# Pair sums held in a PSUM bank, and two gate results in one bank

## Chip, cores and metric

The kernel runs on one core of a Trainium2 chip. The metric is the device time of one execution in microseconds (us); lower is better. The work is split over TensorE (PE, with its weight loads as PEld), VectorE (DVE), ScalarE (ACT), GpSimd (POOL) and the DMA queue that SyncE issues (SP).

## What is computed

Three stages follow one another: a recurrent attention over 768 steps (4 batches, 8 heads, 48 wide), a soft mixture of 8 experts with 32 slots, and a bilinear layer. The last two, cut to what matters here:

```python
slot_out = ...                                # 32 slots x 384, from the experts
x = c @ slot_out                              # c: 3072 tokens x 32 slots (softmax)
a, b = x @ w_a, x @ w_b                       # 384 -> 1536
return (a * b) @ w_out                        # 1536 -> 384, 3072 tokens
```

## The kernel before, in words

A token's x is a mix of 32 slots, so `a*b` of a token is a quadratic form in its 32 weights `c`. The kernel therefore never makes `a` and `b` for 3072 tokens. It makes them for the 32 slots, forms the products of pairs of slots, multiplies those by `w_out` once, and at the end multiplies each block of 128 tokens' pair weights by that small result.

**Gates.** `Gates.products` (line 852) multiplies the experts' output by the two weight matrices in three thirds m = 0, 1, 2. `Gates.turned` (line 869) transposes one third on TensorE into a PSUM tile `pt` (256 numbers per partition), which ScalarE copies into SBUF (line 876), with a small VectorE copy of the first 16 columns (line 877). Each of the three tiles has a bank of its own, tags `g0`, `g1`, `g2` in banks 5, 6 and 7 (line 1279).

**Pair sums.** There are 12 of them, f = 0 to 11, four from each third. Each is a chain over four engines:

- `Sums.pairs(f)` (line 906) forms two products of 128x512 at line 914: `z` on VectorE, from the gate's PSUM tile and its SBUF copy, and `z2` on POOL, from the SBUF copy alone (for f = 0 both are on VectorE). `z` has three SBUF buffers, `z2` two.
- `Sums.add(f)` (line 938): VectorE adds `z2` to `z`, in place in SBUF.
- `Sums.round(f)` (line 943): ScalarE rounds the sum to the short format, `zh` (three buffers).
- `Sums.second(f)` (line 949): VectorE subtracts `zh` from the sum, which gives the remainder `zl` (two buffers).
- `Sums.product(f)` (line 963): TensorE adds twelve 128x384 matmuls (`zh` and `zl` with the two parts of `w_out`) into four PSUM banks.

The order on each queue is the order in which the program emits it. `Sums.run` (line 966) emits for i = 0 to 11: `pairs(i+2)`, `second(i+1)`, `add(i+2)`, `round(i+2)`, what stands beside it, then `product(i)`. The first two sums are started by hand (lines 1286 to 1302). What stands beside (line 1309) is, for i = 2, 4, 6, three small POOL products (`Sums.rest`, lines 925 to 927); for i = 3, 5, 7 their eight small matmuls (line 933); for i = 7, 8, 9, 11 a step of `Pairs.rest` (ScalarE copies at line 1001, then POOL adds at lines 1004 and 1005, ScalarE copies at line 1008); for i = 6, 9 the VectorE product at line 1050 and for i = 7, 10 its split (ScalarE line 1062, VectorE lines 1063 and 1064), which prepare the first two blocks of tokens.

**Output.** `Pairs.take` (lines 1022 to 1028) splits the sums' result, and `Pairs.product` (line 1090) makes 24 blocks of 128 tokens with 13 matmuls each (lines 1098, 1101, 1102), in banks 5, 6 and 7, with a copy (line 1105) and a store (line 1106).

Of the kernel before, what the change touches and what calls it, by code (L numbers as in the profile page):

```python
# [7 lines left out]
F32 = mybir.dt.float32  # L8
# [5 lines left out]
ALU = mybir.AluOpType  # L14
# [38 lines left out]
class Slots:  # L53


    def __init__(self, pool):
        self.pool, self.n = pool, 0
# [12 lines left out]
class Carve:  # L70
# [5 lines left out]
    def add(self, area, *spec):  # L76
        if isinstance(area, list):
            for a, s in zip(area, spec):
                self.add(a, *s)
            return self  # L80
        o = 0
        for tag, n, bufs in spec:
            for _ in range(bufs):
                self.views.setdefault(tag, []).append(area[:, o:o + n])
                o += n
        assert o <= area.shape[1], (o, spec)
        return self
# [693 lines left out]
def experts(nc, sh, k, siT, scale, sb, ps, wq, soT, step):  # L781
# [14 lines left out]
    for r in range(2):  # L796
        for j in range(4):
            e = 4 * r + j
            w = wq.tiles[e]
            hp = ps.tile([128, 256], F32, tag="p", name="hp")  # L800
            for kb in range(KB):
                for q in range(4):
                    nc.tensor.matmul(out=hp[32 * q:32 * q + NS, :], lhsT=siT[:, kb, :], rhs=w[q][:, kb, :],
                                     start=(kb == 0), stop=(kb == KB - 1))
            wq.done(e)
            h = sb.tile([128, 256], F32, tag="h", name="h")
            nc.scalar.activation(out=h, in_=hp, func=ACTF.Relu, scale=scale)
            if late:
                turned(*late.pop())
            late.append((r, j, h))  # L810
            step(e)
# [32 lines left out]
class Gates:  # L844
# [2 lines left out]

    def __init__(self, nc, sh, k, sb, soT, ws):
        self.nc, self.sh, self.k, self.sb, self.soT, self.ws = nc, sh, k, sb, soT, ws
        self.a, self.p, self.g = {}, {}, {}  # L850

    def products(self, ps, m):

# [15 lines left out]
    def turned(self, ps, m):  # L869
        nc, NS = self.nc, self.sh.NS  # L870
        a = self.a.pop(m)
        self.p[m] = pt = ps.tile([128, 2, 4, NS], F32, tag=f"g{m}", name="pt")
        for i in range(2):
            nc.tensor.transpose(out=pt[:, i], in_=a[:, i, :], identity=self.k["ident"])
        self.g[m] = g = self.sb.tile([128, 2, 4, NS + 16], F32, tag="gate", name="gate")
        nc.scalar.activation(out=g[:, :, :, 0:NS], in_=pt, func=ACTF.Copy)
        nc.vector.tensor_copy(out=g[:, :, :, NS:NS + 16], in_=pt[:, :, :, 0:16])
# [8 lines left out]
class Sums:  # L886
# [47 lines left out]
                             start=(m == 0), stop=(m == 2))  # L934

    def add(self, f):
        z, z2 = self.st[f]
        self.nc.vector.tensor_tensor(out=z, in0=z, in1=z2, op=ALU.add)

    def round(self, f):  # L940
        z, _ = self.st[f]
# [246 lines left out]
def kernel(  # L1188
# [39 lines left out]
    def post(k, siT, scale, wq, slots, wab, wo_sb, banks, sb, pairs, chore):  # L1228
        ps = banks.again(p=(4, 5, 6, 7), wm=(0, 1))
        chore = chore(ps)  # L1230
        free = [(5, 5), (6, 6), (7, 7), (8, 8), (9, 9), (11, 10), (3, 14), (4, 15)]
        sums = Sums(nc, sh, k, wo_sb, sb)

        warm = k["ident"].bitcast(BF16)

        def keep(n):

            if n:
                t = ps.tile([128, 256], F32, tag="wm", name="warm")
                for _ in range(n):  # L1240
                    nc.tensor.matmul(out=t, lhsT=warm[:, 0:128], rhs=warm, start=True, stop=True)

        def step(e, last=None):

            while free and wq.used > free[0][1]:
                i = free.pop(0)[0]
                if i in (6, 7, 8):
                    sums.rooms += [[s[:, j * DM:(j + 1) * DM].bitcast(F32R) for j in range(2)]
                                   for s in slots.quarters(i)]
                elif i == 9:  # L1250
                    sb.add(slots.take(i), ("cab", 2304, 1), ("f", 640, 1))
                    pairs.ncab, pairs.nf = 1, 1
                elif i == 11:
                    sb.add(slots.take(i), (("ga", 384, 2),), (("gate", 384, 2),), (("gate", 384, 1), ("o", 384, 1)),
                           (("o", 384, 2),))
                elif i == 3:
                    sb.add(slots.take(i), ("cab", 2304, 1), ("f", 640, 1))
                    pairs.ncab, pairs.nf = 2, 2
                else:
                    s = slots.quarters(i)  # L1260
                    pairs.rooms += [s[0:2], s[2:4]]
            if last:
                keep(KEEP[e])
                last()
            if e == 1:
                pairs.moe.keep(sh.NG - 1, ps, "p")
            if e > 6:
                sums.split()
                sums.split()
            if e in (8, 13):  # L1270
                next(chore, None)
            if not last:
                keep(KEEP[e])

        sb.add(pairs.moe.acc_room[:, 0:KB * sh.NS], ("soT", KB * sh.NS, 1))
        soT = sb.tile([128, KB, sh.NS], F32, tag="soT", name="soT")
        experts(nc, sh, k, siT, scale, sb, ps, wq, soT, step)
        pairs.loads(soT)
        ps = banks.again(p=(0, 1, 2), g0=(5,), g1=(6,), g2=(7,))
        sb.add(slots.take(10), ("r1", 1536, 1))  # L1280
        sb.add(slots.take(0), ("zh", 512, 3), ("zl", 512, 2), ("tr", 384, 1))
        sb.add(slots.take(1), ("z", 512, 3), ("z2", 512, 2), ("zr", 64, 2))
        gates = Gates(nc, sh, k, sb, soT, wab)
        sums.gates = gates
        pairs.blank()
        part = [gates.products(ps, m) for m in range(3)]
        next(part[0])
        next(part[0])
        next(part[1])
        gates.turned(ps, 0)  # L1290
        sums.pairs(0)
        next(part[1])
        next(part[2])
        sums.add(0)
        gates.turned(ps, 1)
        next(part[2])
        sums.round(0)
        sums.pairs(1)
        sums.second(0)
        sums.add(1)  # L1300
        gates.turned(ps, 2)
        sums.round(1)
        ps = banks.again(tp0=(0,), tp1=(1,), tp2=(2,), tp3=(3,), tp4=(4,))
        tp = [ps.tile([128, DM], F32, tag=f"tp{m}") for m in range(5)]
        sb.add(wab[0].rearrange("p k f -> p (k f)"), ("f", 640, 2), ("cab", 2304, 1))
        pairs.ncab, pairs.nf = 3, 4
        last = pairs.rest(tp[4])

        def beside(n):
            sums.split()  # L1310
            if n in (2, 4, 6):
                sums.rest(n // 2 - 1)
            if n in (3, 5, 7):
                sums.rest_product(n // 2 - 1, tp[4])
            if n in (7, 8, 9, 11):
                next(last, None)
            if n in LATER:
                getattr(pairs, LATER[n])()

        sums.run(tp, beside)  # L1320
        for _ in last:
            pass
        sb.add(slots.take(2), ("th", 1536, 1), ("tl", 1536, 1))
        pairs.take(tp)
        ps = banks.again(yo=(5, 6, 7))
        pairs.ahead(2)
        pairs.product((0, 1), ps)
        for n in range(2, pairs.n):
            pairs.ahead(2)
            pairs.product((n,), ps)  # L1330
# [3 lines left out]
    with tc.manual_schedule(), ExitStack() as fast:  # L1334
# [3 lines left out]
        banks = Banks(fast.enter_context(tc.tile_pool(name="banks", bufs=1, space=PSUM)),  # L1338
                      tp=TPB, A=AB, y=(5, 6), misc=(7,))
        ps = banks  # L1340
# [46 lines left out]
        for n in range(NU + 1):  # L1387
# [5 lines left out]
            if n >= 1:  # L1393
                g = (n - 1) // 2
# [6 lines left out]
            if 3 <= n < NU:  # L1401
                if n % 2:
                    g = (n - 3) // 2
# [6 lines left out]
            if PRE[0] <= n < PRE[1]:  # L1410
                m = 4 * NPRE * (n + 1 - PRE[0]) // (PRE[1] - PRE[0]) - 4 * NPRE * (n - PRE[0]) // (PRE[1] - PRE[0])
# [9 lines left out]
            if n == NU - 1:  # L1421
# [7 lines left out]
        rest(sb2, slots)  # L1429
        pairs = Pairs(nc, sh, k, moe, sb2, out)  # L1430
        post(k, siT, scale, wq, slots, wab, wo_sb, banks, sb2, pairs,
             lambda ps: range_flag(nc, sh, k, pool, moe, att, flag, ps))

    val = nc.values_load(flag, min_val=0, max_val=1)
    with tc.If(val > 0):
        with ExitStack() as slow:
# [5 lines left out]
            banks = Banks(slow.enter_context(tc.tile_pool(name="sbanks", bufs=1, space=PSUM)), tp=(0, 1), misc=(2, 3, 4), p=(5, 6, 7))  # L1442
# [23 lines left out]
            rest(sb2, slots)  # L1466
            pairs = Pairs(nc, sh, k, moe, sb2, out)
            post(k, siT, scale, wq, slots, wab, wo_sb, banks, sb2, pairs, lambda ps: iter(()))


# [28 lines left out]
```

## Time and profile before

| | us |
|---|---|
| median of 3 runs | 392.18 (391.66 to 392.22) |
| the profiled execution | 391.77 |
| its span, first to last instruction | 390.0 |
| busy: PE / PEld / DVE / ACT / POOL | 336.3 / 265.6 / 308.2 / 227.5 / 181.2 |

The span is what the rows of the trace divide; the profiled execution's own time is 1.77 us longer than its span, and 0.41 us below the median. Of the span, the stretch from 0 to 288 us is attention and experts, 288 to 328.5 the gates and pair sums, and from there to the end the output. A row of the timeline gives start, duration, engine, line, operation, output and inputs, shapes, and in brackets how long the engine had been idle and what released it.

### The profile page before, as it was taken

The page shows a single profiled execution, that of the slowest core. Times are in us where ns is not written, and L with a number is a line of the kernel's source. Part 1 is how long each engine was busy: PE and PEld are TensorE (multiplying, and loading weights), DVE is VectorE, ACT ScalarE, POOL GpSimd, SP SyncE. Part 2 cuts the span into 40 slices and gives each one's busy share as a digit, 9 for nine tenths or more (in the row PEclk, how much of TensorE's full clock was granted, in tenths as well). Part 3 has the DMA queues.
Part 4 walks back from the last instruction along what each step waited for, and adds up shares of the span by engine and source line. Part 5 has one row for each costly group of instructions (what it writes and reads, how often), then busy time and mean ns, then how long its engine had stood idle before and what let it go on. Part 6 is the DMA issues. An engine that isn't in the chain of part 4 may idle for free.

```text
span 390.0 us, 9985 instructions
## 1 busy us (share of the span) xinstructions
PE 336.3 (86%) x3634; PEld 265.6 (68%) x3634; DVE 308.2 (79%) x616; ACT 227.5 (58%) x672; POOL 181.2 (46%) x224
## 2 busy tenths in 40 slices
PE   7595979988878979878879988899989969999993
PEld 3364767767756858757757776554457759998993
DVE  2476999999999998999999975425349979877850
ACT  4277687795976957966966855335232235544451
POOL 5263776676666566675666651000026734222200
PEclk9689889999999869989989989999999999999999
DMA  7669797879979668979668998799859100899422
GB/s 124 123 116 261 158 210 192 203 151 235 255 152 218 183 118 201 253 160 231 164 127 190 257 294 255 229 366 376 288 130 215 24 0 2 229 270 305 142 90 69
DMA packets 138634, 73.75 MB, mean 189 GB/s; under 512 B 105328, under 2 KB 133104, under 8 KB 138576
## 3 DMA queue, kind: packets, MB, share of 16 engines
q1 hardware_dynamic: 137424, 69.48, 71.2%
q0 software_dynamic: 1152, 3.54, 2.7%
q8 instruction: 31, 0.51, 0.6%
q14 instruction: 27, 0.22, 0.2%
HBM read 67.68 MB, written 5.31 MB: 187 GB/s over the span
## 4 chain that ended last, share of the span: by engine, by line
DVE 49%; PE 24%; DMA 13%; issue 6%; SPq 4%; ACT 3%; POOL 0%; DVEq 0%; ACTq 0%; POOLq 0%
DMA s<-in_moe_w_dram 8%; DVE s L534 8%; DVE s L529 7%; PE yo L1098 6%; DVE s L583 6%; DVE s L712 5%; DVE wab L714 4%; DVE s L551 3%; PE yo L1101 3%; SPq L489 3%; DVE wo L714 2%; PE tp L579 2%; DVE s L683 2%; PE tp L963 2%; PE y L680 2%
## 5 line engine op out<-in xcount | busy, mean ns | idle before, releaser
L505 PE MATMUL tp<-ident,s 128*128 128x128 f32 x288 | 50.0, 298 | 7.7 <-ACT s L593 3.8
L579 PE MATMUL tp<-s,s 64*128 64x128 f32 x384 | 37.2, 298 | 18.9 <-DVE s L610 9.5
L579 PEld LDWEIGHTS tp<-s,s 64*128 64x128 f32 x384 | 30.2, 197 | 24.0 <-issue 21.7
L554 POOL TENSOR_TENSOR s<-s,s 128x384 f32<-128x384 f32 x32 | 37.4, 1190 | 18.5 <-DVE s L551 18.5
L505 PEld LDWEIGHTS tp<-ident,s 128*128 128x128 f32 x288 | 33.5, 148 | 18.1 <-issue 6.0
L647 ACT ACTIVATE s<-s,s 128x48 f32<-128x48 f32 x192 | 45.7, 324 | 0.2
L547 POOL TENSOR_TENSOR s<-s,s 128x384 f32<-128x384 f32 x30 | 36.7, 1238 | 15.7 <-DVE s L534 10.0
L583 DVE TENSOR_TENSOR s<-tp,s 128x384 f32<-128x384 f32 x64 | 32.4, 545 | 9.4 <-PE tp L579 9.2
L529 DVE TENSOR_TENSOR_SCAN s<-s,s 128x387 f32<-128x387 f32 x32 | 33.1, 1072 | 7.0 <-ACT s L510 7.0
L1098 PE MATMUL yo<-s,s 128*128 128x384 f32 x192 | 37.8, 338 | 0.4 <-DVE s L1063 0.4
L534 DVE TENSOR_TENSOR_SCAN s<-s,s 128x387 f32<-128x387 f32 x32 | 35.0, 1121 | 0.5
L680 PEld LDWEIGHTS y<-s,s 128*64 128x64 f32 x768 | 29.0, 156 | 9.0 <-issue 8.7
L1098 PEld LDWEIGHTS yo<-s,s 128*128 128x128 f32 x192 | 33.7, 188 | 1.2 <-DVE s L1063 1.0
L963 PE MATMUL tp<-s,s 128*128 128x384 f32 x144 | 29.8, 358 | 5.2 <-DVE s L949 4.5
L680 PE MATMUL y<-s,s 128*64 128x48 f32 x768 | 33.2, 243 | 0.0
L963 PEld LDWEIGHTS tp<-s,s 128*128 128x128 f32 x144 | 25.9, 198 | 10.0 <-DVE s L949 7.0
L512 ACT ACTIVATE s<-tp 128x384 f32<-128x384 f32 x64 | 30.2, 488 | 2.5 <-PE tp L505 1.7
L717 POOL TENSOR_TENSOR wab<-wab,s 128x384 int32<-128x384 int32 x24 | 27.8, 1160 | 6.3 <-DVE wab L714 2.8
L1105 ACT ACTIVATE s<-yo 128x384 f32<-128x384 f32 x24 | 11.8, 493 | 28.0 <-PE yo L1102 11.9
L1106 POOL DMA_DIRECT2D out_dram<-s x18 | 9.9, 553 | 33.9 <-ACT s L1105 32.0
L712 DVE TENSOR_SCALAR s<-s 128x384 uint32<-128x384 uint32 x36 | 23.2, 644 | 2.9 <-ACT wab L704 2.9
L620 POOL TENSOR_TENSOR s<-s,pc_all 64x288 f32<-64x288 f32 (+1 forms) x32 | 21.2, 663 | 8.1 <-DVE s L610 6.9
(190 smaller groups left out, 738.9 us busy)
## 6 DMA issues: line engine op xcount, KB each, us to landing
s<-in_moe_w_dram SPq DMA_DIRECT2D x64, 384.0 KB, 5.9
s<-in_w_dram SPq DMA_DIRECT2D x48, 96.0 KB, 3.5
s<-in_k_dram SPq DMA_DIRECT2D x48, 96.0 KB, 5.0
s<-in_r_dram SPq DMA_DIRECT2D x48, 96.0 KB, 3.2
s<-in_v_dram SPq DMA_DIRECT2D x48, 96.0 KB, 3.4
s<-in_moe_w_a_dram SPq DMA_DIRECT2D x12, 384.0 KB, 3.9
s<-in_moe_w_b_dram SPq DMA_DIRECT2D x12, 384.0 KB, 4.1
s<-in_moe_w_out_dram SPq DMA_DIRECT2D x12, 384.0 KB, 3.7
```

Of the source, the lines that this page charges most:

```text
L505: nc.tensor.transpose(out=pt[:, c, :], in_=t[:, c, 2 * p:2 * p + 2, :].rearrange("p h d -> p (h d)"), identity=ident)
L529: nc.vector.tensor_tensor_scan(out=P[:, hs[p]], data0=wt[:, hs[p]], data1=self.lo, initial=0.0, op0=ALU.mult, op1=ALU.max)
L534: nc.vector.tensor_tensor_scan(out=suf[:, hs[p]][:, ::-1], data0=wt[:, o + 1:o + H + 1][:, ::-1], data1=d1[:, hs[p]][:, ::-1], initial=0.0 ...
L547: (nc.gpsimd if n else nc.vector).tensor_tensor(out=part(suf, p, 1), in0=part(suf, p, 1), in1=plain(kT, p), op=ALU.mult)
L554: nc.gpsimd.tensor_tensor(out=plain(rT, p), in0=plain(rT, p), in1=plain(kT, p), op=ALU.mult)
L579: nc.tensor.matmul(out=aps[hh][:, c, :], lhsT=K[64 * hh:64 * hh + 64, o + 1:o + 1 + C], rhs=R[64 * hh:64 * hh + 64, o:o + C], start=True, ...
L583: nc.vector.tensor_tensor(out=a, in0=aps[hh], in1=self.mask.unsqueeze(1).to_broadcast([128, 3, C]), op=ALU.mult)
L647: nc.scalar.activation(out=av[:, c, h], in_=V[:, c, h, 0:D], func=ACTF.Copy, scale=a0[:, c, h // 2, h % 2:h % 2 + 1])
L680: nc.tensor.matmul(out=yp[th, c, hh, :], lhsT=am[p, hh][:, c, th], rhs=V[:, c, 2 * p + hh, :], start=False, stop=c == 2 and hh == 1)
L712: nc.vector.tensor_scalar(out=raw[:, :, 1], in0=raw[:, :, 1], scalar1=0x80000000, scalar2=None, op0=ALU.bitwise_and)
L963: nc.tensor.matmul(out=tp[m], lhsT=a[:, m * 128:(m + 1) * 128], rhs=b, start=first and i == 0, stop=last and i == 2)
L1098: nc.tensor.matmul(out=y, lhsT=a[:, m, :], rhs=self.th[:, m, :], start=m == 0 and a is fh, stop=False)
```

## The change

The sum of the two products is written by `add` to a PSUM tile `zs` of one bank (7) in place of the SBUF buffer `z`; `round` and `second` read it there. To free that bank, the gates' tiles of m = 0 and m = 1 become two halves of one tile in bank 5, and that of m = 2 moves to bank 6.

```diff
@@ Gates.turned
-        self.p[m] = pt = ps.tile([128, 2, 4, NS], F32, tag=f"g{m}", name="pt")
+        if m % 2 == 0:
+            self.room = ps.tile([128, 2, 2, 4, NS], F32, tag=f"g{m}", name="pt")
+        self.p[m] = pt = self.room[:, m % 2]
@@ Sums.add
         z, z2 = self.st[f]
-        self.nc.vector.tensor_tensor(out=z, in0=z, in1=z2, op=ALU.add)
+        zs = self.ps.tile([128, 512], F32, tag="z", name="zs")
+        self.nc.vector.tensor_tensor(out=zs, in0=z, in1=z2, op=ALU.add)
+        self.st[f] = zs, None
@@ post
-        ps = banks.again(p=(0, 1, 2), g0=(5,), g1=(6,), g2=(7,))
+        ps = banks.again(p=(0, 1, 2), g0=(5,), g2=(6,), z=(7,))
...
-        sums.gates = gates
+        sums.gates, sums.ps = gates, ps
```

## Rows read from the trace of the kernel before

**Rows 1.** Busy time by stretch: us (instructions) of PE, PEld, DVE, ACT, POOL; clock, DMA.

```profile
291.90:328.50 36.60, 31.77 (x169) 26.50 (x170) 33.07 (x42) 12.75 (x23) 22.02 (x22) 0.95 0.33 68
328.50:390.00 61.50, 55.21 (x313) 54.12 (x311) 40.79 (x70) 26.35 (x48) 9.95 (x18) 0.99 0.61 175
```

**Rows 2.** Timeline of TensorE, pair sums; in brackets idle time before and its releaser.

```profile
299.97 0.84 PE L933 MATMUL tp<-wo,s 128*16 128x384 f32 x8
...
305.46 0.84 PE L933 MATMUL tp<-wo,s 128*16 128x384 f32 x8
...
320.17 5.91 PE L963 MATMUL tp<-s,s 128*128 128x384 f32 x24 [2.77 <-DVE s L949]
326.64 2.00 PE L963 MATMUL tp<-s,s 128*128 128x384 f32 x10 [0.56 <-DVE s L949]
328.48 2.79 PE L1098 MATMUL yo<-s,s 128*128 128x384 f32 x15
```

**Rows 3.** VectorE by line and shape, 287 to 328 us: busy, mean ns | idle before.

```profile
L949 DVE TENSOR_TENSOR s<-s,s 128x512 fp32r<-128x512 f32 x12 | 14.1, 1177 | 1.2 <-ACT s L943 1.1
...
L914 DVE TENSOR_TENSOR s<-s 128x512 f32<-128x512 f32 x1 | 1.2, 1186 | 0.0
```

**Rows 4.** Timeline of VectorE, POOL and ScalarE, add(2) to second(4).

```profile
295.39 0.68 DVE L938 TENSOR_TENSOR s<-s 128x512 f32<-128x512 f32 x1
...
296.22 1.20 POOL L914 TENSOR_TENSOR s<-s 128x512 f32<-128x512 f32 x1 [1.29 <-DVE s L938]
...
299.24 1.21 POOL L914 TENSOR_TENSOR s<-s 128x512 f32<-128x512 f32 x1
299.48 1.52 DVE L949 TENSOR_TENSOR s<-s,s 128x512 fp32r<-128x512 f32 x1 [0.18 <-ACT s L943]
...
300.92 0.68 DVE L938 TENSOR_TENSOR s<-s 128x512 f32<-128x512 f32 x1
...
301.72 0.63 ACT L943 ACTIVATE s<-s 128x512 fp32r<-128x512 f32 x1 [2.27 <-DVE s L938]
...
302.38 1.07 DVE L949 TENSOR_TENSOR s<-s,s 128x512 fp32r<-128x512 f32 x1 [0.18 <-ACT s L943]
```

**Rows 5.** The tile g: VectorE's products with one PSUM input, ns min/median/max.

```profile
L914 DVE TENSOR_TENSOR s<-g,s x12: 675/678/692, 288.7 to 320.6; 128x512 f32<-128x512 f32 x12
```

**Rows 6.** ScalarE by line and shape, 384 columns, from PSUM and from SBUF.

```profile
L512 ACT ACTIVATE s<-tp 128x384 f32<-128x384 f32 x8 | 3.9, 487 | 0.3
...
L903 ACT ACTIVATE s<-wo 128x384 fp32r<-128x384 f32 x12 | 5.1, 510 | 0.0
```

**Rows 7.** Timeline around the second transposes and the first remainder, 288 to 293 us.

```profile
288.69 0.69 DVE L914 TENSOR_TENSOR s<-g,s 128x512 f32<-128x512 f32 x1
...
289.28 0.44 PE L874 MATMUL g<-ident,s 128*128 128x128 f32 x2
...
291.12 0.28 DVE L877 COPY s<-g 128x128 f32<-128x128 f32 x1
...
291.92 1.11 DVE L949 TENSOR_TENSOR s<-s,s 128x512 fp32r<-128x512 f32 x1
```

**Rows 8.** Timeline of VectorE and POOL, the last pair sums.

```profile
313.86 1.10 DVE L949 TENSOR_TENSOR s<-s,s 128x512 fp32r<-128x512 f32 x1
...
319.44 0.68 DVE L949 TENSOR_TENSOR s<-s,s 128x512 fp32r<-128x512 f32 x1
...
324.56 1.48 POOL L1005 TENSOR_TENSOR s<-s 16x384 f32<-16x384 f32 x1
325.09 1.49 DVE L949 TENSOR_TENSOR s<-s,s 128x512 fp32r<-128x512 f32 x1
```

**Rows 9.** The chain that ended last: TensorE's rate in the output stage.

```profile
337.77 1.39 PE yo L1098 x8
339.16 0.69 PE yo L1101 x4
```

**Rows 10.** Busy time by stretch, as rows 1, one stretch after TensorE's long idle time.

```profile
320.00:321.00 1.00, 0.83 (x3) 0.83 (x4) 1.00 (x3) 0.16 (x1) 0.00 (x0) 0.50 0.00 0
```

More of the change, by code (lines that the diff above doesn't have):

```diff
@@ L849, in __init__ @@
         self.nc, self.sh, self.k, self.sb, self.soT, self.ws = nc, sh, k, sb, soT, ws
-        self.a, self.p, self.g = {}, {}, {}
+        self.a, self.p, self.g, self.room = {}, {}, {}, {}
     def products(self, ps, m):
```

## The prediction

> **What bounds the kernel now.** I read the busy time by stretch first. In the output stage TensorE is busy 55.2 of 61.5 us and nothing of the change lies there; in the pair sums, 36.6 us long, VectorE is busy 33.1 us and TensorE 31.8 us [rows 1]. A matmul's pipelined end counts as busy, so I take TensorE's need from its rate in the output stage: 8 in 1.39 us and 4 in 0.69 us, 0.174 us each [rows 9]. The twelve sums need 144 x 0.174 = 25.1 us and the three groups of eight small ones, whose pitch is 0.77 us (0.84 less the overlap of its end), 2.3 us: 27.4 of 36.6 us. So some 9 us are waits, and the timeline names for the long ones the remainder of line 949 on VectorE [rows 2]. The group of TensorE's small matmuls recurs after 305.46 - 299.97 = 5.49 us, where 24 x 0.174 + 0.77 = 4.95 us would do [rows 2, 9].
>
> VectorE by line then shows which of its three instructions per sum is odd. The remainder (line 949) costs 1.177 us on average, and the one product that VectorE makes from two SBUF inputs 1.186 us [rows 3]; a sum (line 938) that meets no POOL work takes 0.68 us, and so does a remainder after POOL has fallen silent [rows 4, 8]. The timeline shows why: POOL's product runs from 299.24 to 300.45 us, the remainder begun at 299.48 us ends at 301.00 us, 0.55 us after POOL [rows 4]. An instruction that reads two SBUF inputs stands still until POOL's product is done. VectorE's twelve products with one PSUM input span only 675 to 692 ns, whether POOL works or not [rows 5].
>
> **The change, part by part.** 1. *The remainder reads the sum from PSUM.* It then has the inputs of line 914, one in PSUM and one in SBUF, so I price it at 0.68 us [rows 5]. On VectorE alone that is 14.1 - 12 x 0.68 = 5.9 us [rows 3, 5].
>
> Not all of it shortens the chain, since the sum (line 938) still reads two SBUF inputs and now meets POOL instead. Sum(f) starts POOL's product f+2. Where POOL has no small products, VectorE's next sum comes, after 0.12 us to ScalarE's start, some 0.6 us of rounding, 0.03 us and a remainder's pitch of 0.60 us, 1.35 us after the last sum; POOL's 1.20 us product, begun 0.08 to 0.15 us after that sum, has just ended. So the first two remainders give their full 1.11 - 0.68 = 0.43 us each [rows 7], together 0.86 us. In the next six sums POOL also makes the small products, every second time. From the end of one sum (296.07) to POOL's start is 0.15 us, to its next product 299.24 - 296.22 = 3.02 us, that product takes 1.21 us, and a sum held by it ends about 0.55 us later: 4.93 us, against 301.60 - 296.07 = 5.53 us now [rows 4]. Three such pairs give 3 x 0.60 = 1.8 us. TensorE's 4.95 us would allow no more. Remainder 8 goes from 1.10 to 0.68, 0.42 us; 9 and 10 run beside an idle POOL (0.68 us already) and give nothing; 11 goes from 1.49 to 0.68, 0.81 us, as POOL's addition at 324.56 no longer holds it [rows 8]. Sum: 0.86 + 1.8 + 0.42 + 0.81 = 3.9 us.
>
> What is late next is TensorE. The wait for remainder 9 (2.77 us idle) moves forward with it by 0.86 + 1.8 + 0.42 = 3.1 us but stays as long, because between remainders 8 and 9 VectorE sits behind a split of line 1063 that waits for ScalarE. TensorE's 24 matmuls after it then have only the 0.56 us of idle at 326.64 to give [rows 2]: 3.1 + 0.56 = 3.7 us. [...]
>
> 2. *The sum is written to PSUM.* No VectorE instruction of the trace writes there, so I bound it. The nearest row is line 914, where a PSUM input in place of an SBUF one changes nothing (678 against 680 ns). Above, I allow what a held instruction adds, 1.19 - 0.68 = 0.51 us [rows 3]; below, a gain of 0.02 us, what ScalarE shows between the two memories [rows 6]. I take 0. TensorE sets the end by 0.2 us, so 12 x 0.02 us is all the first end could give; the other is the rival on the slow side.
>
> [...]
>
> 3. *ScalarE rounds from PSUM.* 487 against 510 ns at 384 columns [rows 6]: 0.02 us of 0.63 per sum, inside the rounding of the terms above.
>
> 4. *One sum buffer in place of three.* Sum(f) must wait for the rounding and remainder of f-1. Both stand ahead of it on VectorE's queue already (the remainder itself waits for the rounding), so no instruction waits that did not: 0. POOL still starts after the sum that frees its `z2`, and nothing on SP or POOL is moved.
>
> 5. *Two gates' results in one bank.* If engines are kept apart by bank, the transposes of the second third, now at 289.28 us, wait for the product with the first third to end at 289.38 us [rows 7]: about 0.1 us on TensorE. ScalarE's copy moves with them, but VectorE wants it only at 291.12 us, behind its first sum, and TensorE waits for the first rounding anyway. Cost 0; without that cover 0.1 us. Bank 7 is next used by the third output block, long after remainder 11.
>
> The profiled execution gives 391.77 - 3.7 = 388.1 us. It stands 0.41 us below the median of 392.18, so on the median's scale: 388.5 us.
>
> **The rivals.**
> *A, the forecast*, as above: 388.5.
> *B, the sums don't meet POOL.* If POOL's second product ends before the sum arrives, or holds it only briefly, the whole 5.9 us of the remainders count: 392.2 - 5.9 = 386.3. For it: TensorE's 9 us of waits leave room. Against: the 3.02 us between POOL's starts put its product under the sum.
> *C, writing to PSUM costs a little.* At 0.1 to 0.2 us a sum, 1.2 to 2.4 us go on VectorE's chain: 389.7 to 390.9. For it: no row shows the write.
> *D, the remainder is still held by POOL*, through its other input: the change doesn't do what it is for, only ScalarE's 0.02 us a sum stays, 391.9. Against it stand line 914's twelve even durations, one SBUF input among theirs.
> *E, slower: the write to PSUM is dear.* Place: line 938, on the chain of every sum. It decides from 3.7 / 12 = 0.31 us a sum; at the bound of 0.51 us it is 12 x 0.51 = 6.1 us, 388.5 + 6.1 = 394.6. For it: unseen, and VectorE is the bound here. Against: nothing in the reading direction costs anything like it.
>
> **How the numbers follow.** A 0.50, B 0.18, C 0.13, D 0.10, E 0.09. About 0.2% (0.78 us) is what a measurement of this kernel can tell from no change. A, B and C are faster by more: 0.81; D is within it: 0.10; E slower: 0.09. The range takes in A with its terms' errors, B and most of C: 386.1 to 391.0; what it leaves out is D, E and the far end of C, some 2 in 10.
>
> **What the next profile would show.** Line 949 with inputs named for a PSUM tile, twelve alike near 0.68 us; were they spread up to 1.5 us, D is right and my reading of the holding is wrong. Line 938 at 0.68 us where POOL is idle (0.8 or more everywhere would be C, 1.2 E), and some three of them at 1.2 us or more under a POOL product; if none, B. TensorE's small matmuls should recur after about 4.95 us, its long idle time should stand some 3 us earlier at the same length, and the first output matmul should start near 324.8 us with the output stage unchanged at about 61.5 us. If that stage grows, a cause I have not named took the gain.

## The result, and the profile after

The changed kernel takes 387.94 us (median of 4 runs, 387.84 to 389.08) against 392.12 us before (391.66 to 392.22): ratio 0.9903, 95% interval 0.9874 to 0.9932, faster by 4.2 us.

The profiled execution of the changed kernel took 389.08 us, with a span of 387.4 us: only 2.7 us less than the one before. In it the pair sums begin late: VectorE's copy of line 817, the last step of the experts, starts at 286.29 us where it started at 285.10 us before. Over all the runs below that start lies between 283.9 and 287.1 us, in code that none of them changes. So I measure what the change touches by the **stretch** from that copy to the first output matmul. Before it was 328.48 - 285.10 = 43.38 us.

The timeline of TensorE, pair sums, changed kernel (compare [rows 2]; line 968 is the old 963, 935 the old 933, 1103 the old 1098):

```profile
293.08 7.12 PE L968 MATMUL tp<-s,s 128*128 128x384 f32 x36 [0.17 <-ACT s L948]
300.13 0.84 PE L935 MATMUL tp<-wo,s 128*16 128x384 f32 x8
300.90 4.45 PE L968 MATMUL tp<-s,s 128*128 128x384 f32 x24
305.28 0.84 PE L935 MATMUL tp<-wo,s 128*16 128x384 f32 x8
...
317.75 4.60 PE L968 MATMUL tp<-s,s 128*128 128x384 f32 x24 [1.75 <-DVE s L954]
323.77 2.01 PE L968 MATMUL tp<-s,s 128*128 128x384 f32 x10 [1.42 <-DVE s L954]
325.73 3.08 PE L1103 MATMUL yo<-s,s 128*128 128x384 f32 x16
```

The stretch is now 325.73 - 286.29 = 39.44 us, shorter by 3.94 us. The small matmuls recur after 5.15 us in place of 5.49, the first long wait is 1.75 us in place of 2.77, and the last one has grown from 0.56 to 1.42 us. The output stage takes 387.4 - 325.7 = 61.7 us, as before [rows 1].

The new PSUM tile z, all that writes and reads it (ns min/median/max), and VectorE and ScalarE by line and shape (busy, mean ns | idle before), 285 to 326 us:

```profile
L942 DVE TENSOR_TENSOR z<-s x12: 699/700/855, 291.7 to 320.0; 128x512 f32<-128x512 f32 x12
L948 ACT ACTIVATE s<-z x12: 597/599/607, 292.4 to 320.9; 128x512 fp32r<-128x512 f32 x12
L954 DVE TENSOR_TENSOR s<-z,s x12: 677/690/693, 293.1 to 323.0; 128x512 fp32r<-128x512 f32 x12
```

```profile
L942 DVE TENSOR_TENSOR z<-s 128x512 f32<-128x512 f32 x12 | 8.7, 724 | 1.2
L954 DVE TENSOR_TENSOR s<-z,s 128x512 fp32r<-128x512 f32 x12 | 8.2, 686 | 1.0 <-ACT s L948 0.9
```

The remainder (line 954) fell from 1177 to 686 ns [rows 3] and is even; the sum rose from 712 to 724 ns; the rounding fell from 632 to 600 ns. New is an idle time of 1.2 us ahead of the sums, for which the view names no releaser.

The timeline of VectorE and POOL over one pair of sums, changed kernel (compare [rows 4]):

```profile
296.08 0.70 DVE L942 TENSOR_TENSOR z<-s 128x512 f32<-128x512 f32 x1
...
296.93 1.22 POOL L916 TENSOR_TENSOR s<-s 128x512 f32<-128x512 f32 x1 [1.05 <-DVE z L942]
297.45 0.69 DVE L954 TENSOR_TENSOR s<-z,s 128x512 fp32r<-128x512 f32 x1
298.10 0.32 POOL L927 TENSOR_TENSOR s<-s 128x64 f32<-128x64 f32 x1
298.25 0.73 DVE L942 TENSOR_TENSOR z<-s 128x512 f32<-128x512 f32 x1
298.38 0.77 POOL L928 TENSOR_TENSOR s<-s 128x64 f32<-128x64 f32 x1
...
299.51 1.21 POOL L916 TENSOR_TENSOR s<-s 128x512 f32<-128x512 f32 x1
...
300.52 0.75 DVE L942 TENSOR_TENSOR z<-s 128x512 f32<-128x512 f32 x1
```

The remainder at 297.45 us runs through POOL's product untouched (0.69 us). From the remainder's start to the next sum's it is 298.25 - 297.45 = 0.80 us although the remainder lasts 0.69. POOL's second product starts 2.58 us after the first, not 3.02 as before, and the sum at 300.52 us, begun under its end, is held by a few hundredths only (0.75 us where an unheld one takes 0.70).

### The profile page after: what moved, and what is told of

Read it like the earlier page. It is cut to its first block, busy times and chain, and to the rows that moved or that the text cites. A ratio compares the mean times of both kernels' runs of the same rounds, so it can differ in the third digit from the quotient of the medians.

```text
span 387.4 us, 9985 instructions
## 1 busy us (share of the span) xinstructions
PE 336.3 (87%) x3634; PEld 265.7 (69%) x3634; DVE 303.2 (78%) x616; ACT 226.8 (59%) x672; POOL 179.3 (46%) x224
## 4 chain that ended last, share of the span: by engine, by line
DVE 51%; PE 23%; DMA 12%; issue 5%; SPq 4%; ACT 3%; POOL 0%; DVEq 0%; ACTq 0%; POOLq 0%
DVE s L534 8%; DVE s L529 8%; DMA s<-in_moe_w_dram 6%; DVE s L583 6%; PE yo L1103 6%; DVE s L712 5%; DVE s L551 4%; DVE wab L714 4%; PE tp L968 3%; PE yo L1106 3%; SPq L489 3%; DVE s L683 2%; DVE wo L714 2%; DVE s L610 2%; PE tp L579 2%
## 5 line engine op out<-in xcount | busy, mean ns | idle before, releaser
L579 PE MATMUL tp<-s,s 64*128 64x128 f32 x384 | 38.6, 304 | 17.8 <-DVE s L610 9.5
L579 PEld LDWEIGHTS tp<-s,s 64*128 64x128 f32 x384 | 31.1, 201 | 23.1 <-issue 20.8
L968 PE MATMUL tp<-s,s 128*128 128x384 f32 x144 | 27.3, 343 | 3.5 <-DVE s L954 3.2
L968 PEld LDWEIGHTS tp<-s,s 128*128 128x128 f32 x144 | 24.5, 188 | 7.1 <-DVE s L954 4.5
```

The lines of the kernel that those rows point to most:

```text
L579: nc.tensor.matmul(out=aps[hh][:, c, :], lhsT=K[64 * hh:64 * hh + 64, o + 1:o + 1 + C], rhs=R[64 * hh:64 * hh + 64, o:o + C], start=True, ...
L968: nc.tensor.matmul(out=tp[m], lhsT=a[:, m * 128:(m + 1) * 128], rhs=b, start=first and i == 0, stop=last and i == 2)
```

## The experiments

Each ran in 5 rounds beside the kernel before on the same chip; ratios are to that. The stretch is from each run's own profile, one per kernel. The three kernels whose sums stay in SBUF beside POOL's products (before, banks alone, filled wait) have 43.38, 43.34 and 43.37 us, so it repeats far better than the whole time: the ratios of the runs without POOL's products and with two banks (0.989 to 0.990) can't be told from the 0.9903 of the changed kernel, their stretches can.

**The banks alone.** `Gates.turned` and the bank list as in the change, the sums left in SBUF:

```diff
-        ps = banks.again(p=(0, 1, 2), g0=(5,), g1=(6,), g2=(7,))
+        ps = banks.again(p=(0, 1, 2), g0=(5,), g2=(6,))
```

> The kernel before, with the gates of m = 0 and 1 in one bank and nothing else of the change. The measure in all runs is the stretch from VectorE's copy of line 817 (acc from p) to the first output matmul: 43.4 us before, 39.4 us after the change. My theory (the gain comes from the remainder's PSUM input alone, the shared bank is free): stretch 43.4 +- 0.3, time within 0.2% of before, the transposes of the second third start 0.1 us after the first product ends. Rival (the banks matter by themselves): stretch off by 0.5 us or more.

Measured: 0.9989 (0.9964 to 1.0013), stretch 329.09 - 285.75 = 43.34 us; the second transposes start 290.17 - 290.02 = 0.15 us after the first product ends. Sharing a bank costs and gives nothing here.

**Who holds the remainder.** The kernel before, and then the changed one, without POOL's products: from f = 1 on every sum adds the z2 of f = 0.

```diff
-        for eng, o, a, b in ((nc.vector, z, Bp, A), (nc.gpsimd if n else nc.vector, z2, A, B)):
+        for eng, o, a, b in ((nc.vector, z, Bp, A), (nc.vector, z2, A, B))[:1 if n else 2]:
```

> The kernel before, sums in SBUF, but POOL's eleven products z2 are left out (the product of f = 0 is added every time), so POOL does not read SBUF while VectorE works except for the small products. Theory (POOL's SBUF reads hold a VectorE instruction with two SBUF inputs): line 949 falls from 1.18 to about 0.69 us with both inputs still in SBUF, and the stretch from 43.4 to 37.5 to 39.5 us, as short as with the change or shorter; time 386 to 388.5. Rival (a PSUM input is quicker by itself, POOL has no part): line 949 stays at 1.1 us or more, the stretch above 42.5 us.

Measured: 0.9893 (0.9862 to 0.9924), stretch 324.99 - 286.62 = 38.37 us. In the timeline of VectorE the remainder (here line 951, both inputs still in SBUF) takes 0.68 or 0.69 us ten times of twelve; the exceptions, 0.82 and 1.48 us, stand in the program beside POOL's small products and its addition at the end:

```profile
299.16 0.69 DVE L951 TENSOR_TENSOR s<-s,s 128x512 fp32r<-128x512 f32 x1 [0.18 <-ACT s L945]
299.77 0.68 DVE L940 TENSOR_TENSOR s<-s 128x512 f32<-128x512 f32 x1
...
301.23 0.82 DVE L951 TENSOR_TENSOR s<-s,s 128x512 fp32r<-128x512 f32 x1 [0.18 <-ACT s L945]
...
321.62 1.48 DVE L951 TENSOR_TENSOR s<-s,s 128x512 fp32r<-128x512 f32 x1
```

So the remainder needed no PSUM for its 0.69 us, only POOL out of its way: the rival that a PSUM input is quicker by itself is out. Here a sum starts 0.61 us after the remainder ahead of it.

> The changed kernel with the same eleven POOL products left out. Theory (with the change POOL hardly holds VectorE any more): the remainder stays at 0.69 us, the sums fall from 0.72 to 0.70 us, the stretch is 38.6 to 39.4 us, and not shorter than that of the kernel before without POOL's products, because the sum now waits for the remainder in front of it. Rival (a good part of the holding has only moved to the sums): the stretch falls below 38 us.

Measured: 0.9898 (0.9850 to 0.9946), stretch 322.34 - 283.90 = 38.44 us, a little under what I gave. Of the 1.0 us to the changed kernel, 0.5 us is VectorE's own second product for f = 0 (0.68 us in place of 1.19, as in the run before it), which I had left out of account; 0.5 us is what POOL still costs the changed kernel. As expected it is no shorter than the run before it.

**The wait ahead of the sums.** Two banks in turn: the gates of m = 1 and 2 share bank 6, so bank 5 is free from f = 4 on; bank 4 serves until the small matmuls take it.

```diff
-        zs = self.ps.tile([128, 512], F32, tag="z", name="zs")
+        zs = self.ps.tile([128, 512], F32, tag="z" if f < 4 else "zz", name="zs")
...
-        ps = banks.again(p=(0, 1, 2), g0=(5,), g2=(6,), z=(7,))
+        ps = banks.again(p=(0, 1, 2), g0=(5,), g1=(6,), z=(7, 4), zz=(5, 7))
```

> The changed kernel with two banks for the sum in turn (7 and 4, then 5 and 7; the gates of m = 1 and 2 share bank 6, the rest product takes bank 4 only when it starts). In the changed kernel a sum starts 0.78 us after the remainder in front of it, before the change 0.60 us where nothing held it. Theory (the sum overwrites the bank that the remainder is still reading, and waits for it to end): 0.60 us again, 12 x 0.18 = 2.2 us less on VectorE, of which 0.3 to 1.3 us show in the stretch (38.1 to 39.1 us), as TensorE is close to its limit. Rival (it is the price of writing to PSUM): 0.78 us stays, stretch 39.4 us.

Measured: 0.9889 (0.9847 to 0.9931), stretch 322.36 - 284.12 = 38.24 us, 1.2 us less than with one bank. The timeline of VectorE and POOL:

```profile
294.89 0.69 DVE L954 TENSOR_TENSOR s<-z,s 128x512 fp32r<-128x512 f32 x1
295.50 0.69 DVE L942 TENSOR_TENSOR z<-s 128x512 f32<-128x512 f32 x1
...
297.00 1.20 POOL L916 TENSOR_TENSOR s<-s 128x512 f32<-128x512 f32 x1
297.54 1.21 DVE L942 TENSOR_TENSOR zz<-s 128x512 f32<-128x512 f32 x1
```

A sum starts 0.61 us after the remainder again, with the write to PSUM unchanged. So the 0.18 us went with the single buffer. Not all of it is the buffer's by itself: in the run without POOL's products, with one bank, it is 295.50 - 294.77 = 0.73 us. Why POOL's products add some 0.06 us to the wait is not shown.

```profile
294.77 0.69 DVE L956 TENSOR_TENSOR s<-z,s 128x512 fp32r<-128x512 f32 x1
295.50 0.70 DVE L944 TENSOR_TENSOR z<-s 128x512 f32<-128x512 f32 x1
```

With two banks the sum of f = 4 comes sooner, meets POOL's product and takes 1.21 us, ending 0.55 us after it (297.54 and 297.00 us in the timeline above): the holding that the prediction had charged to the changed kernel.

**The waits that are left.** The two subtractions of the first block's split (lines 1068 and 1069 of the changed kernel) are emitted beside i = 8 in place of 7:

```diff
+        def small():
+            nc.vector.tensor_tensor(out=fl, ...)
+            nc.vector.tensor_tensor(out=fr[32:64], ...)
...
+            if n == 8:
+                pairs.due()
```

> The changed kernel, with the two VectorE subtractions of the first block's split emitted one step later (beside i = 8 in place of 7), so that VectorE does not stand behind them while ScalarE makes their input. Theory (after the change the largest wait left is this one: VectorE idle 2.23 us, TensorE idle 1.75 us before the second part of the sums): the remainder of sum 9 comes some 2 us sooner, TensorE's idle time there falls below 0.3 us, the stretch from 39.4 to 37.4 to 38.4 us. Rival (TensorE's matmuls or ScalarE's copies give the wait back): stretch above 39.0 us.

Measured: 0.9859 (0.9818 to 0.9899), stretch 322.90 - 285.54 = 37.36 us. TensorE runs 48 matmuls of the sums without a gap where it had stood for 1.75 us; two shorter waits are left:

```profile
310.47 8.60 PE L968 MATMUL tp<-s,s 128*128 128x384 f32 x48
319.63 0.62 PE L968 MATMUL tp<-s,s 128*128 128x384 f32 x2 [0.56 <-ACT s L948]
321.05 2.02 PE L968 MATMUL tp<-s,s 128*128 128x384 f32 x10 [0.80 <-DVE s L954]
```

> Two banks for the sums and the late subtractions together. Theory: the gains add up as far as TensorE allows, stretch 36.4 to 37.6 us, and TensorE waits only for the remainder of sum 11, which stands behind VectorE's product of line 1055 (2.46 us, held by POOL's addition). Rival (TensorE is the bound already with one of the two): stretch as in the better one alone.

Measured, with both edits: 0.9825 (0.9786 to 0.9863), stretch 321.98 - 285.25 = 36.73 us, one wait left (0.81 us, for remainder 11).

**A version faster than both.** Both edits, and VectorE's product for the second block one step sooner:

```diff
-LATER = {6: 'more', 7: 'half', 9: 'more', 10: 'half'}
+LATER = {6: 'more', 7: 'half', 8: 'more', 10: 'half'}
```

> As the run with two banks and late subtractions, and VectorE's product for the second block one step sooner (beside i = 8 in place of 9), ahead of POOL's addition. Theory (that product is held by POOL's addition and the remainder of sum 11 behind it): it takes 0.8 to 1.0 us in place of 2.46, TensorE has no wait left, and its own need sets the stretch: 6.8 us to the first matmul and 144 x 0.183 + 2.3 = 28.6 us, 35.4 to 36.6 us in all. Rival (ScalarE's and POOL's steps for the rest then set the start of the output stage): stretch above 36.8 us, with the wait in front of the first output matmul.

Measured: 385.66 us against 392.78 beside it, 0.9816 (0.9779 to 0.9854); stretch 322.01 - 286.00 = 36.01 us. The product takes 0.82 us in place of 2.46, and TensorE goes into the output stage without a wait (timeline of TensorE, then of VectorE):

```profile
310.74 11.44 PE L968 MATMUL tp<-s,s 128*128 128x384 f32 x60
322.01 2.27 PE L1108 MATMUL yo<-s,s 128*128 128x384 f32 x12
...
314.40 0.82 DVE L1055 TENSOR_TENSOR s<-s 128x640 f32<-128x640 f32 x1
```

**The clock.** Sixteen small matmuls in TensorE's long wait of the kernel before:

```diff
             beside(i)
+            if i == 9:
+                self.warm()
             self.product(i, tp)
```

> The kernel before, with 16 small bf16 matmuls into an idle bank ahead of the matmuls of sum 9, so that TensorE is not idle for 2.8 us there and its clock need not fall. Theory (the fall to half the clock costs nothing, since the remainder of sum 11 comes last anyway): the granted clock stays at 1.00 and the 24 matmuls take some 4.6 us in place of 5.9, but the wait for sum 11 grows by as much and the stretch stays 43.4 +- 0.3 us. Rival (a part of the change's gain is the clock that no longer falls): stretch 42.0 to 42.8 us.

Measured: 1.0004 (0.9974 to 1.0033), stretch 330.51 - 287.14 = 43.37 us. Timeline of TensorE, then the busy time by stretch (the third number from the end is the granted clock):

```profile
322.21 4.50 PE L963 MATMUL tp<-s,s 128*128 128x384 f32 x24 [1.04 <-DVE s L949]
328.67 2.00 PE L963 MATMUL tp<-s,s 128*128 128x384 f32 x10 [1.96 <-DVE s L949]
```

```profile
322.00:326.00 4.00, 3.79 (x21) 3.78 (x22) 3.82 (x6) 2.24 (x4) 1.41 (x1) 1.00 0.00 0
```

The 24 matmuls take 4.50 us in place of 5.91 [rows 2], the granted clock is 1.00 where [rows 10] has 0.50, and the wait for remainder 11 grows by the same 1.4 us. The fall of the clock cost the kernel before nothing.

## Why the prediction was right, step by step

The forecast was 388.5 us and the time is 387.94. The gain forecast for the stretch was 3.7 us (terms of 3.9, of which TensorE would take back 0.2), and it shortened by 3.94. But two terms were wrong, in opposite directions (2 and 3 below), and that they nearly cancel is luck. The same terms, from the two profiles (starts of the sums, ends of the remainders):

| part | forecast | measured |
|---|---|---|
| sum 0 to sum 2 | 0.86 | 4.88 - 4.38 = 0.50 |
| sum 2 to sum 8 | 1.8 | 16.53 - 13.62 = 2.91 |
| sum 8 to remainder 9 | 0.42 | 8.20 - 8.00 = 0.20 |
| remainder 9 to remainder 11 | 0.81 | 6.46 - 6.02 = 0.44 |
| to the first output matmul | -0.2 | 1.90 - 2.01 = -0.11 |
| all | 3.7 | 3.94 |

1. *The remainder at 0.68 us* was right (686 ns), and its reason is shown: POOL's work on SBUF held it. Without POOL's products the remainder takes 0.68 or 0.69 us ten times of twelve with both inputs in SBUF; with POOL's products and the sum in PSUM, the changed kernel's twelve take 677 to 693 ns. The sum of 1.21 us in the run with two banks still has two SBUF inputs; started under POOL's product, it ends 0.55 us after it. Rival D is out.

2. *The pairs with POOL's small products* were mis-sized: 2.91 us, not 1.8. I took the 3.02 us between POOL's starts from the profile before as POOL's own. But the small products there were held by VectorE as well: the first starts under a remainder, the second under a sum, and each takes 0.77 us, where the first takes 0.32 us in the changed kernel. The timeline of VectorE and POOL, kernel before:

```profile
296.77 1.20 DVE L949 TENSOR_TENSOR s<-s,s 128x512 fp32r<-128x512 f32 x1
297.39 0.77 POOL L925 TENSOR_TENSOR s<-s 128x64 f32<-128x64 f32 x1
297.89 0.80 DVE L938 TENSOR_TENSOR s<-s 128x512 f32<-128x512 f32 x1
298.11 0.77 POOL L926 TENSOR_TENSOR s<-s 128x64 f32<-128x64 f32 x1
```

POOL by line and shape (busy, mean ns), the two products before, then after the change (line 927 is the old 925, 928 the old 926):

```profile
L925 POOL TENSOR_TENSOR s<-s 128x64 f32<-128x64 f32 x3 | 2.3, 773 | 0.0
L926 POOL TENSOR_TENSOR s<-s 128x64 f32<-128x64 f32 x3 | 2.3, 768 | 0.0
...
L927 POOL TENSOR_TENSOR s<-s 128x64 f32<-128x64 f32 x3 | 1.0, 325 | 0.0
L928 POOL TENSOR_TENSOR s<-s 128x64 f32<-128x64 f32 x3 | 1.9, 640 | 0.0
```

The third, POOL's addition of the two (old line 927), rose from 325 to 432 ns. With the remainder out of POOL's way, POOL is done sooner, and the sum is hardly held. With 2.58 us for the 3.02, the forecast's own steps come out: 0.15 + 2.58 + 1.21 + 0.55 = 4.49 us, and from the end of sum 2 to that of sum 4 it is 301.27 - 296.78 = 4.49 us. That this explains all of the 1.1 us is argued from these rows, not isolated in a run.

By the prediction's own signs this speaks for rival B: not one sum took the 1.2 us that A wanted of some three, the twelve took 699 to 855 ns. B's 14.1 - 8.2 = 5.9 us of the remainders came too. Its 386.3 us did not, because of the wait in 3, which neither A nor B had: 11 x 0.18 = 2.0 us, which leaves 3.9. A's number was met by another route than A's.

3. *One buffer in place of three* was put at 0 because the remainder stands ahead of the sum anyway. The step missed that standing ahead is not the same as having ended. Two VectorE instructions in a row overlapped here: the next started 0.60 us into one of 0.68. The sum that overwrites the bank its neighbour reads started only after that neighbour's end: a remainder of 0.68 us starts at 293.11 us in the changed kernel, the sum behind it at 293.89, 0.78 us later. That is 0.18 us per sum, and it is why the first, third and fourth rows of the table fall short. The two banks took it away.

4. *The write to PSUM* costs 0.02 us at most: the median sum is 700 ns where 0.68 us was taken, 0.68 to 0.70 over two banks where POOL does not hold it. The rivals C and E are out: the 0.18 us of 3 has the size that C gave, but it is not the price of the write: with two banks the write stays, and a sum starts 0.61 us after the remainder. The input from PSUM costs nothing either: the median remainder is 690 ns with it, and 0.69 us from SBUF alone where POOL's products are left out.

5. *TensorE would take back 0.2 us, after a wait as long as before.* The wait was 1.75 us, not 2.77, and the granted clock after it was 1.00 where [rows 10] has 0.50: 24 matmuls took 4.60 us. Busy time by stretch, as in [rows 1]:

```profile
318.00:321.00 3.00, 3.00 (x18) 2.79 (x18) 2.74 (x5) 1.71 (x4) 0.70 (x1) 1.00 0.00 0
```

Counted from the copy of line 817, remainder 9 ends 3.6 us sooner, but TensorE's matmuls ahead of it only 2.6 us sooner: TensorE's need was put too low, 4.95 us from one group of small matmuls to the next where it took 5.15. TensorE still waited for remainder 11 in the end (1.42 us) and took nothing back. That the clock stayed at 1.00 gained nothing in itself, as far as the filled wait shows it for the kernel before (stretch 43.37 us against 43.38).

6. *The banks of the gates* cost nothing, as forecast: the second transposes waited 0.17 us for VectorE (0.1 was forecast), and the run with the banks alone has the stretch of before.

## What to carry to other kernels

If two-input VectorE instructions of one kind last now 0.7 and now 1.5 us, as the remainders did here, look at what POOL does meanwhile. Here an input moved to PSUM brought all twelve to 0.68 or 0.69 us, and POOL's two small products fell with them, from 773 to 325 and from 768 to 640 ns on average. Price a buffer that goes from several to one even where the order on the queue already has the reader first: here the overlap of the two neighbours went with it, 0.18 us a sum. And compare kernels by the stretch that was changed, when the time ahead of it varies by as much as the gain.

## What the runs showed of the hardware that I had not expected

Holding went both ways: a POOL product of 64 columns took 0.32 us when it started ahead of a VectorE sum (298.10 us above) and 0.77 us when it started under one (298.38 us). TensorE's matmuls of the sums came every 0.183 us without any wait between (24 in 4.38 us) where the same shape took 0.174 us in the output stage [rows 9]; no run here tells why, and it is what bounds the fastest version: 144 x 0.183 + 2.3 = 28.7 us of the 29.2 us from its first sum matmul to its first output matmul.
